# A three-layer kernel: the last two rows in another order, closing products by pair, conversions of the last layer placed elsewhere

## The chip, the cores and the metric

One core of one Trainium2 chip. The metric is the device time of one launch in microseconds (us), as the median of several runs; the profile is of one further execution. The engines have the names of the profile: PE (TensorE, matmuls), ACT (ScalarE), DVE (VectorE), POOL (GpSimd), SP (SyncE, which here only issues DMAs). PSUM is the memory that matmuls write to, in eight banks. Each engine works through its own instructions in the order in which the program issues them; what an instruction needs from another engine it waits for, and everything behind it on its engine waits too.

## The reference

Three layers, one behind the other. A delta-rule attention over 4 batches, 8 heads, 768 positions, heads of 48:

```python
for t in range(S):
    kt, vt, bt = (k_n[:, :, t], v[:, :, t], beta[:, :, t, None])
    y[:, :, t] = np.einsum('bhd,bhde->bhe', q[:, :, t], state)
    v_old = np.einsum('bhde,bhd->bhe', state, kt)
    state = state + bt[:, :, :, None] * np.einsum('bhd,bhe->bhde', kt, vt - v_old)
```

Its output, 3072 tokens of 384, goes through a gated layer of width 1536 (with an RMS norm ahead):

```python
g = xn @ w_gate
silu = g * (1.0 / (1.0 + np.exp(-g)))
return (silu * (xn @ w_val) @ w_out).astype(np.float32)
```

and that through a layer of width 2048 with h * tanh(softplus(h)) between its two products:

```python
h = x @ w_in
sp = np.where(h > 20.0, h, np.log1p(np.exp(np.minimum(h, 20.0))))
return ((h * np.tanh(sp)) @ w_out).astype(np.float32)
```

## The kernel before

**Products in three parts.** Every large product is taken as three matmuls: a number is split into a high part (rounded to the type of the fast fp32 matmul) and a low part (the rest), and high x high, high x low, low x high are summed in PSUM. So each operand exists as a pair of tiles: xh and xl, hh and hl, gh and gl, and wh and wl for each weight.

**Conversions.** The weights arrive as 64-bit floats. `prepare_half` (L150) turns one half of a weight block (128 x 384) into high and low parts, in steps between which other work is issued: a DMA to `raw` (four buffers); an abs pass into `t` (three buffers), on ACT (L166) or, with `act=False`, on DVE (L168); a pair of DVE passes (L170, L173); a second pair (L178, L181); then a cast to the high part, on ACT (L192) or DVE (L194), and the subtraction that gives the low part (L195), on the engine `low`, which is POOL unless a caller says otherwise. The subtraction is the last reader of `t`, so the abs pass three halves later waits for it. `convs` (L199) runs many halves one behind the other, overlapped by a step, and yields a weight for each step: 1.5 for each half, 0.3 at the start.

**Order by merging.** The program's order of issue is made by generators. `merge` (L61) takes streams with a total each and always continues the one whose done share of its total is smallest; `budget` (L71) ends a stream after an amount of weight; `run` issues streams one behind the other. A total that is larger than the stream's true weight lets it run ahead of the others.

**Phase b1: attention and the first third of the gated layer.** The sequence is worked through in 12 rows of 64 positions (256 tokens over the batches). `chain_row` (L891) issues one row as named stages: r (residual with the state), q0 and q1 (transposes of q), p (scores), y (output from the state), v (values: its results are copied by ACT into `ve`, L965, and it then loads the next row's v on SP, L395), k (update of the state sx, L1014; nothing in the last row), o0 and o1 (outputs: a product of `ve` and the scores into two banks, ACT copies `po`, L984, a sum of squares, and POOL's norm `rv`, L996), s0 and s1 (a diagonal matrix `dg` from `rv` on ACT, L1022), x0 and x1 (product with `dg`, L1036, six ACT copies to xh and xf, L1040 and L1042, POOL's xl, L1043; x1 also stores xh and xl to DRAM by SP). The capitals S, T, X, Y are s0, s1, x0, x1 of the row before, which the list of a row may place among its own stages. `ROW` is the list of rows 3 to 11; n, c and g prepare row r + 4 and issue nothing in the last four rows. Behind row 11 its own s0, s1, x0, x1 are issued by `run` (L1190).

Among the stages of row r the merge places 11 units of `part_a`, the gated layer on two pairs of weight blocks (`FA` = 2, L1135), some blocks behind the attention, and, in rows 10 and 11, conversions of the other weights. `gated` (L258): for each block of 256 tokens and each pair of weights four units (two pg, two pv, nine matmuls each), ACT's silu (L289), DVE's product sg and cast hh (L295, L298), POOL's hl (L299). Behind the first pair of a block come the closing products of the block before: `down` (L262), 12 matmuls for each of three output slices o, over both pairs of weights, then a copy of the slice by ACT (`par`, L1092). The slices use one PSUM bank in the rows, and three from L1192 on. Behind row 11 22 units are left ("the turns" below); they are merged with the conversions (L1194).

**Phase b2: the other pairs of the gated layer** (`phase_b2`, L1200), with the rest of the conversions of the last layer's weights but five (L1238 to 1241). The five, w_out2 blocks 3 to 7, are prepared with `act=False` and started in the last 14 units (L1244), up to an amount `CVC`.

**Phase c: the last layer** (`phase_c`, L1248). Units (n, m): 18 matmuls into a bank ph, ACT's sigmoid, arctan and sine, DVE's product t (L1307) and cast gh (L1310), POOL's gl (L1311). Units go in batches of three, the first batch before the last closing products of b2. Six banks hold ph; DVE's product t frees one. Behind each batch conversions of weight `CVD` are issued. `down` (L1254) closes a block of eight units with 96 matmuls, and needs all eight w_out2 blocks.

Of the kernel before, what the change touches and what calls it, by code (L numbers as in the profile page):

```python
# [8 lines left out]
F32 = mybir.dt.float32  # L9
# [8 lines left out]


P = dict(  # L20
    XB=2, WE=16, RB=4, TB=3, LANE=15.7, CVT=12.22, CVB0=0, CVB1=1.238, CVC=2.31, PSD=1, NU=6, CVA=1, CVE=14.671, CVD=4.076, SQ=5,
    ROW="r nA q0 q1 S p T nB y X v Y k c0 o0 c1 o1 g".split(),
    R0="r q0 q1 p v k o0 o1 s0 s1 x0 x1 c0 c1 g".split(),
    R1="r nA q0 q1 y p nB v k o0 o1 s0 s1 x0 c0 c1 g".split(),
    R2="r nA Y q0 q1 p nB y v k c0 o0 c1 o1 g".split(),
    DUE=[0, 6, 5, 11],
    CVS=[0, 0, 6.5, 0],
    C=dict(n=0.2, q=0.5, r=1.4, y=1.1, p=1.2, v=1.2, o=0.9, k=1.2, s=0.1, x=0.45, c=0.4, d=0.4, g=1.2, h=1.2),
# [69 lines left out]
def kernel(  # L98
# [14 lines left out]
    nc = tc.nc  # L113
    B, H, S, D = q.shape
    NT, DM = out.shape
# [142 lines left out]
    def gated(pools, pairs, blocks, get_x, finish_of, ahead=lambda n: None, between=lambda: None):  # L258
        ps_u, ps_d, hp, tp = pools
        pairs = list(pairs)  # L260

        def down(hs, finish):  # L262
            for o in range(KD):
                ps = ps_d[-1].tile([128, DM], F32, tag="d", name="pd")[:, 0:T]
                sl = slice(o * 128, (o + 1) * 128)
                for i, m in enumerate(pairs):
                    wh, wl = W["o", m]
                    hh, hl = hs[i]
                    for f in range(2):
                        last = i == len(pairs) - 1 and f == 1  # L270
                        nc.tensor.matmul(ps, wh[:, f, sl], hh[:, f, :], start=(i + f == 0), stop=False)  # L271
                        nc.tensor.matmul(ps, wh[:, f, sl], hl[:, f, :], start=False, stop=False)  # L272
                        nc.tensor.matmul(ps, wl[:, f, sl], hh[:, f, :], start=False, stop=last)  # L273
                    if i % 2 == 1 and i < len(pairs) - 1:
                        yield 1
                finish(o, ps)
                yield 1

        prev = None
        for n in blocks:  # L280
            hs = []
            for m in pairs:
                xh, xl = get_x(n)
                pg = ps_u.tile([128, 2, T], F32, tag="u", name="pg")
                up(pg, W["g", m], 0, xh, xl)
                yield 1
                up(pg, W["g", m], 1, xh, xl)
                sg = tp.tile([128, 2, T], F32, tag="sg", name="sg", bufs=2)
                nc.scalar.activation(out=sg, in_=pg, func=ACTF.Silu)  # L289
                yield 1  # L290
                pv = ps_u.tile([128, 2, T], F32, tag="u", name="pv")
                up(pv, W["v", m], 0, xh, xl)
                yield 1
                up(pv, W["v", m], 1, xh, xl)
                nc.vector.tensor_tensor(out=sg, in0=sg, in1=pv, op=ALU.mult)  # L295
                hh = hp.tile([128, 2, T], F32R, tag="hh", name="hh")
                hl = hp.tile([128, 2, T], F32R, tag="hl", name="hl")
                nc.vector.tensor_copy(hh, sg)  # L298
                nc.gpsimd.tensor_tensor(out=hl, in0=sg, in1=hh.bitcast(F32), op=ALU.subtract)  # L299
                hs.append((hh, hl))  # L300
                yield 1
                if m == pairs[0] and prev is not None:
                    yield from down(*prev)
                if m == pairs[1]:
                    ahead(n + 1)
            done.add(("up", n))
            prev = hs, finish_of(n)
        between()
        yield from down(*prev)

    def x_tiles():
        return [xp.tile([128, KD, T], F32R, tag=tag, name=tag, bufs=XB) for tag in ("xh", "xl")]
# [7 lines left out]
    def phase_b1():  # L320
# [759 lines left out]
            return P["C"][LATE.get(name, name)[0]]  # L1080

        def order(r):
            return P[f"R{r}"] if r < 3 else P["ROW"]

        def cost(r):
            return sum(cost_of(x) for x in order(r))
# [71 lines left out]
        for sg in range(1, NSEG):  # L1158
            for rl in range(2):
                r = 2 * sg + rl  # L1160
                streams = [(chain_row(r), cost(r))]
                due = P["DUE"][r] if r < len(P["DUE"]) else P["DUE"][-1]
                if due > 0:
                    off = 1.5 if r == 2 else 0
                    streams.append((seq(delay(off), budget(part_a, due)), off + due))
                if r < len(P["CVS"]):
                    streams.append((budget(cv, P["CVS"][r]), P["CVS"][r]))
                if r < len(P["CVS"]):
                    streams.append((budget(cv, P["CVS"][r]), P["CVS"][r]))
                if sg + 1 < NSEG:  # L1170
                    upto = (r - 1) * P["LANE"] - 1.5 if r < NR - 3 else 999.0
                    streams.append((until(lane, laned, upto), P["LANE"]))
                elif rl == 0:
                    st_i.close()
                    streams.append((seq(left.pop(), delay(7.0)), 13.0))
                    wbp.append(st_b.enter_context(pool("wbA")))
                    todo = [(c, m, cols(w, m)) for m in range(FA, NP1) for c, w in (("g", w_gate), ("v", w_val))]
                    todo += [("o", m, rows(w_out1, m)) for m in range(FA, NP1)]
                    gens = []
                    for i, (c, m, cut) in enumerate(todo):  # L1180
                        if 2 * i < WE:
                            gens.append(prepare(lambda: wbp[0], (c, m), cut, tag="wb", bufs=WE))
                        else:
                            gens.append(prepare(lambda: wbp[1], (c, m), cut, tag="wb", bufs=2 * len(todo) - WE))
                    cv = convs(gens)
                    streams.append((budget(cv, 0.75 * WE), 0.75 * WE))
                else:
                    streams.append((budget(cv, 0.75 * WE), 0.75 * WE))
                merge(*streams)
        run(*[late[x]() for x in LATE.values() if x in late])  # L1190
        st_a.close()
        ps_ds.append(st_p.enter_context(pool("ps_t", 3, space=PSUM)))  # L1192
        wbp.append(st_w.enter_context(pool("wbB")))
        merge((part_a, 22.0), (budget(cv, P["CVT"]), P["CVT"]))  # L1194
        st_p.close()
        st_m.close()
        return cv
# [2 lines left out]
    def phase_b2(cv, between):  # L1200
        st = ExitStack()
        op = st.enter_context(pool("op2", 1, side="right"))
        hp = st.enter_context(pool("hp2", NP1 - FA + 1, side="right"))
        tp = st.enter_context(pool("tp2", side="right"))
        pars = {}

        def load_par(n, o):
            pars[n, o] = op.tile([128, T], F32, tag="par", name="par", bufs=3)
            nc.scalar.dma_start(out=pars[n, o], in_=p_d[n][:, o, :])

        def next_x(n):
            if n < NR:
                load_x(n)
            else:
                load_x(0, (yh_d, yl_d))

        def finish_b(n):
            for o in range(KD):
                load_par(n, o)
            yh = op.tile([128, KD, T], F32R, tag="yh", name="yh")  # L1220
            yl = op.tile([128, KD, T], F32R, tag="yl", name="yl")

            def finish(o, ps):
                y = pars.pop((n, o))
                nc.vector.tensor_tensor(out=y, in0=y, in1=ps, op=ALU.add)
                nc.vector.tensor_copy(yh[:, o, :], y)
                nc.gpsimd.tensor_tensor(out=yl[:, o, :], in0=y, in1=yh[:, o, :].bitcast(F32), op=ALU.subtract)
                if o == KD - 1:
                    nc.sync.dma_start(out=yh_d[n], in_=yh.bitcast(F32))
                    nc.sync.dma_start(out=yl_d[n], in_=yl.bitcast(F32))  # L1230

            return finish

        more = [prepare(lambda: w2i, ("i", m), cols(w_in2, m)) for m in range(NP2)]
        more += [prepare(lambda: w2i, ("q", m), rows(w_out2, m)) for m in range(QE)]
        cv = seq(cv, convs(more))
        nb = NP1 - FA
        part_b = gated((ps_u, [ps_d], hp, tp), range(FA, NP1), range(NR), lambda n: xs[n], finish_b, next_x, between)  # L1238
        total = NR * 4 * nb + (NR - 1) * 6 - 4 * nb + 8
        merge((budget(part_b, 6), 6), (budget(cv, P["CVB0"]), 6))  # L1240
        merge((budget(part_b, total - 6), total), (cv, P["CVB1"] * 2.9 * (len(more) + 1)))
        cv = convs([prepare(lambda: wbp[0], ("q", m), rows(w_out2, m), act=not P["CVA"], tag="wb", bufs=WE) for m in range(QE, NP2)])
        rest.append(cv)
        merge((part_b, 4 * nb - 2), (budget(cv, P["CVC"]), P["CVE"]))  # L1244
        st.close()
# [122 lines left out]
```

## Time and profile before

| | us |
|---|---|
| median of 3 runs | 1226.76 (1225.94 to 1229.17) |
| the profiled execution | 1225.7 |
| its span, first to last instruction | 1224.0 |
| PE busy | 1128.9 (92%) |
| DVE busy | 707.6 (58%) |
| ACT busy | 566.8 (46%) |
| POOL busy | 418.1 (34%) |

The profile is of one execution. A busy time counts what an engine worked on; a line gives the engine, the line of the kernel, the tile written and the tiles read. An idle time in square brackets is that of the engine before the instruction, with what ended it. The granted clock is a mean over a stretch of the PE clock, as a share of 2.4 GHz; the chip has two levels, 2.4 and 1.2 GHz.

### The profile page before, as it was taken

What the parts mean: (1) busy time and instruction counts of PE and PEld (TensorE: products, weight loads), DVE (VectorE), ACT (ScalarE), POOL (GpSimd) and SP (SyncE); (2) the same over time, 40 slices, a digit from 0 to 9 for tenths busy, and PEclk for the clock granted to TensorE, in tenths of its full rate; (3) what the DMA queues carried; (4) which work ended last, traced back from release to release, by engine and by line L of the source; (5) the groups of instructions that cost most, each with busy time, mean ns of one, the idle gap of its engine ahead of it and who ended that gap; (6) DMA issues with size and microseconds to landing.
All of it is one profiled execution on the core that took longest, in us unless ns stands there. A gap on an engine that the chain in (4) does not pass through costs nothing.

```text
span 1224.0 us, 33707 instructions
## 1 busy us (share of the span) xinstructions
PE 1128.9 (92%) x14784; PEld 1098.7 (90%) x14784; DVE 707.6 (58%) x1130; ACT 566.8 (46%) x1075; POOL 418.1 (34%) x378
## 2 busy tenths in 40 slices
PE   5687698999998778999999999988999999999998
PEld 5676687989898678999999999988999999999998
DVE  6656898788877758455555542357434433343333
ACT  4355645565656563211211111163757555555672
POOL 2031135354322445334434442234323332232232
PEclk7666798999898989999999999998999999999999
DMA  9022233333224543434333231421111101111101
GB/s 159 3 67 67 80 80 67 81 88 85 55 80 119 144 143 130 130 116 143 104 118 103 86 110 65 142 91 52 40 39 40 40 14 39 40 40 39 37 4 27
DMA packets 120484, 95.08 MB, mean 78 GB/s; under 512 B 79856, under 2 KB 102896, under 8 KB 120336
## 3 DMA queue, kind: packets, MB, share of 16 engines
q1 hardware_dynamic: 108240, 69.32, 21.0%
q10 hardware_dynamic: 12096, 23.60, 5.8%
q8 instruction: 116, 1.90, 0.6%
q14 instruction: 32, 0.26, 0.1%
HBM read 64.59 MB, written 28.31 MB: 76 GB/s over the span
## 4 chain that ended last, share of the span: by engine, by line
PE 69%; DVE 18%; ACT 5%; issue 4%; POOL 2%; SPq 1%; DMA 1%; DVEq 0%; POOLq 0%; ACTq 0%
PE pd L1264 5%; PE pd L1265 5%; PE pd L1263 5%; PE ph L256 5%; PE ph L255 5%; PE ph L254 5%; PE pd L271 4%; PE pd L272 3%; PE pd L273 3%; PE pg L254 3%; PE pv L254 3%; PE pg L255 3%; PE pg L256 3%; PE pv L256 3%; PE pv L255 3%
## 5 line engine op out<-in xcount | busy, mean ns | idle before, releaser
L1311 POOL TENSOR_TENSOR gl<-t,gh 128x512 fp32r<-128x512 f32 x96 | 125.2, 1304 | 252.9 <-DVE gh L1310 237.6
L299 POOL TENSOR_TENSOR hl<-sg,hh 128x512 fp32r<-128x512 f32 x72 | 97.3, 1352 | 231.1 <-DVE hh L298 222.4
L254 PE MATMUL ph<-xh,wih 128*128 128x256 f32 x576 | 162.7, 283 | 5.4 <-DVE t L1307 5.4
L255 PE MATMUL ph<-xl,wih 128*128 128x256 f32 x576 | 162.5, 282 | 0.0
L256 PE MATMUL ph<-xh,wil 128*128 128x256 f32 x576 | 162.5, 282 | 0.0
L271 PE MATMUL pd<-hh,woh 128*128 128x256 f32 x432 | 126.0, 292 | 14.8 <-ACT par L1092 12.3
L1263 PE MATMUL pd<-wqh,gh 128*128 128x384 f32 x384 | 130.1, 339 | 1.9 <-DVE wqh L194 1.9
L1264 PE MATMUL pd<-wql,gh 128*128 128x384 f32 x384 | 130.4, 340 | 1.3 <-POOL wql L195 1.3
L1265 PE MATMUL pd<-wqh,gl 128*128 128x384 f32 x384 | 129.9, 338 | 0.0
L254 PE MATMUL pg<-xh,wgh 128*128 128x256 f32 x432 | 128.4, 297 | 0.5 <-ACT wgh L192 0.5
L289 ACT ACTIVATE sg<-pg 128x512 f32<-128x512 f32 x72 | 43.2, 599 | 183.4 <-PE pg L256 162.1
L254 PE MATMUL pv<-xh,wvh 128*128 128x256 f32 x432 | 126.7, 293 | 0.0
L255 PE MATMUL pg<-xl,wgh 128*128 128x256 f32 x432 | 124.1, 287 | 1.7 <-POOL xl L1043 1.7
L272 PE MATMUL pd<-hl,woh 128*128 128x256 f32 x432 | 123.9, 287 | 1.0 <-POOL hl L299 1.0
L256 PE MATMUL pg<-xh,wgl 128*128 128x256 f32 x432 | 123.9, 287 | 0.9 <-DVE wgl L195 0.9
L273 PE MATMUL pd<-hh,wol 128*128 128x256 f32 x432 | 123.6, 286 | 0.0
L255 PE MATMUL pv<-xl,wvh 128*128 128x256 f32 x432 | 122.4, 283 | 0.0
L256 PE MATMUL pv<-xh,wvl 128*128 128x256 f32 x432 | 122.2, 283 | 0.0
L254 PEld LDWEIGHTS ph<-xh,wih 128*128 128x128 f32 x576 | 109.7, 191 | 5.6 <-DVE t L1307 5.6
L295 DVE TENSOR_TENSOR sg<-sg,pv 128x512 f32<-128x512 f32 x72 | 49.2, 684 | 113.3 <-PE pv L256 103.1
L1307 DVE TENSOR_TENSOR t<-t,ph 128x512 f32<-128x512 f32 x96 | 65.2, 679 | 81.8 <-ACT t L1305 81.8
L255 PEld LDWEIGHTS ph<-xl,wih 128*128 128x128 f32 x576 | 109.8, 191 | 0.0
(207 smaller groups left out, 2918.2 us busy)
## 6 DMA issues: line engine op xcount, KB each, us to landing
raw<-in_moe_w_out_dram SPq DMA_DIRECT2D x28, 384.0 KB, 3.5
raw<-in_moe_w_in_dram SPq DMA_DIRECT2D x16, 384.0 KB, 3.8
kh<-in_k_dram SPq DMA_DIRECT2D x24, 192.0 KB, 3.9
qp<-in_q_dram SPq DMA_DIRECT2D x24, 192.0 KB, 3.5
v<-in_v_dram SPq DMA_DIRECT2D x48, 96.0 KB, 3.1
raw<-in_moe_w_gate_dram SPq DMA_DIRECT2D x12, 384.0 KB, 3.2
raw<-in_moe_w_val_dram SPq DMA_DIRECT2D x12, 384.0 KB, 3.4
xh_d<-xh SPq DMA_DIRECT2D x12, 384.0 KB, 2.8
```

The costliest lines, as they stand in the source:

```text
L254: nc.tensor.matmul(ps[:, f, :], wh[:, kt, sl], xh[:, kt, :], start=(kt == 0), stop=False)
L255: nc.tensor.matmul(ps[:, f, :], wh[:, kt, sl], xl[:, kt, :], start=False, stop=False)
L256: nc.tensor.matmul(ps[:, f, :], wl[:, kt, sl], xh[:, kt, :], start=False, stop=(kt == KD - 1))
L271: nc.tensor.matmul(ps, wh[:, f, sl], hh[:, f, :], start=(i + f == 0), stop=False)
L272: nc.tensor.matmul(ps, wh[:, f, sl], hl[:, f, :], start=False, stop=False)
L273: nc.tensor.matmul(ps, wl[:, f, sl], hh[:, f, :], start=False, stop=last)
L299: nc.gpsimd.tensor_tensor(out=hl, in0=sg, in1=hh.bitcast(F32), op=ALU.subtract)
L1263: nc.tensor.matmul(ps, gh[:, f, sl], wh[:, f, :], start=(m + f == 0), stop=False)
L1264: nc.tensor.matmul(ps, gh[:, f, sl], wl[:, f, :], start=False, stop=False)
L1265: nc.tensor.matmul(ps, gl[:, f, sl], wh[:, f, :], start=False, stop=last)
L1307: nc.vector.tensor_tensor(out=t, in0=t, in1=ps, op=ALU.mult)
L1311: nc.gpsimd.tensor_tensor(out=gl, in0=t, in1=gh.bitcast(F32), op=ALU.subtract)
```

## The change

`RL`, a new list of stages, is used in rows 10 and 11. It leaves out the names that issue nothing there, puts Y ahead of v, and o0 ahead of k. The closing products of the last block of part_a are issued by pair of weights: three banks are taken at once, pair 0 is multiplied for all three slices, then pair 1. Behind row 11 come s0 and s1, then three units of part_a, then x0 and x1; the conversions among the turns end earlier (`CVT` 9.0 instead of 12.22, and one weight of nothing behind them), and what is left of them goes into phase b2. For w_out1 blocks 2 to 5 and w_out2 blocks 3 to 7 the low part is made by DVE instead of POOL. In the last 14 units of b2 conversions of weight 4.4 instead of 2.31 are issued, behind a batch of phase c 3.5 instead of 4.076.

```diff
@@ -18,11 +18,12 @@
 
 
 P = dict(
-    XB=2, WE=16, RB=4, TB=3, LANE=15.7, CVT=12.22, CVB0=0, CVB1=1.238, CVC=2.31, PSD=1, NU=6, CVA=1, CVE=14.671, CVD=4.076, SQ=5,
+    XB=2, WE=16, RB=4, TB=3, LANE=15.7, CVT=9.0, CVB0=0, CVB1=1.238, CVC=4.4, PSD=1, NU=6, CVA=1, CVE=14.671, CVD=3.5, SQ=5,
     ROW="r nA q0 q1 S p T nB y X v Y k c0 o0 c1 o1 g".split(),
     R0="r q0 q1 p v k o0 o1 s0 s1 x0 x1 c0 c1 g".split(),
     R1="r nA q0 q1 y p nB v k o0 o1 s0 s1 x0 c0 c1 g".split(),
     R2="r nA Y q0 q1 p nB y v k c0 o0 c1 o1 g".split(),
+    RL="r q0 q1 S p T y X Y v o0 k o1".split(),
     DUE=[0, 6, 5, 11],
     CVS=[0, 0, 6.5, 0],
     C=dict(n=0.2, q=0.5, r=1.4, y=1.1, p=1.2, v=1.2, o=0.9, k=1.2, s=0.1, x=0.45, c=0.4, d=0.4, g=1.2, h=1.2),
@@ -259,6 +260,23 @@
         ps_u, ps_d, hp, tp = pools
         pairs = list(pairs)
 
+        def down_by_pair(hs, finish):
+
+            pss = [ps_d[-1].tile([128, DM], F32, tag="d", name="pd")[:, 0:T] for _ in range(KD)]
+            for i, m in enumerate(pairs):
+                wh, wl = W["o", m]
+                hh, hl = hs[i]
+                for o, ps in enumerate(pss):
+                    sl = slice(o * 128, (o + 1) * 128)
+                    for f in range(2):
+                        last = i == len(pairs) - 1 and f == 1
+                        nc.tensor.matmul(ps, wh[:, f, sl], hh[:, f, :], start=(i + f == 0), stop=False)
+                        nc.tensor.matmul(ps, wh[:, f, sl], hl[:, f, :], start=False, stop=False)
+                        nc.tensor.matmul(ps, wl[:, f, sl], hh[:, f, :], start=False, stop=last)
+                    if i == len(pairs) - 1:
+                        finish(o, ps)
+                    yield 0.5
+
         def down(hs, finish):
             for o in range(KD):
                 ps = ps_d[-1].tile([128, DM], F32, tag="d", name="pd")[:, 0:T]
@@ -306,7 +324,7 @@
             done.add(("up", n))
             prev = hs, finish_of(n)
         between()
-        yield from down(*prev)
+        yield from (down_by_pair if len(pairs) == FA else down)(*prev)
 
     def x_tiles():
         return [xp.tile([128, KD, T], F32R, tag=tag, name=tag, bufs=XB) for tag in ("xh", "xl")]
@@ -1080,7 +1098,7 @@
             return P["C"][LATE.get(name, name)[0]]
 
         def order(r):
-            return P[f"R{r}"] if r < 3 else P["ROW"]
+            return P[f"R{r}"] if r < 3 else P["RL"] if r >= NR - 2 else P["ROW"]
 
         def cost(r):
             return sum(cost_of(x) for x in order(r))
@@ -1181,17 +1199,20 @@
                         if 2 * i < WE:
                             gens.append(prepare(lambda: wbp[0], (c, m), cut, tag="wb", bufs=WE))
                         else:
-                            gens.append(prepare(lambda: wbp[1], (c, m), cut, tag="wb", bufs=2 * len(todo) - WE))
+                            gens.append(prepare(lambda: wbp[1], (c, m), cut, low=nc.vector, tag="wb", bufs=2 * len(todo) - WE))
                     cv = convs(gens)
                     streams.append((budget(cv, 0.75 * WE), 0.75 * WE))
                 else:
                     streams.append((budget(cv, 0.75 * WE), 0.75 * WE))
                 merge(*streams)
-        run(*[late[x]() for x in LATE.values() if x in late])
+        last = [x for x in LATE.values() if x in late]
+        run(*[late[x]() for x in last if x[0] == "s"])
+        run(budget(part_a, 3))
+        run(*[late[x]() for x in last if x[0] == "x"])
         st_a.close()
         ps_ds.append(st_p.enter_context(pool("ps_t", 3, space=PSUM)))
         wbp.append(st_w.enter_context(pool("wbB")))
-        merge((part_a, 22.0), (budget(cv, P["CVT"]), P["CVT"]))
+        merge((part_a, 19.0), (seq(budget(cv, P["CVT"]), delay(1)), P["CVT"] + 1))
         st_p.close()
         st_m.close()
         return cv
@@ -1239,7 +1260,7 @@
         total = NR * 4 * nb + (NR - 1) * 6 - 4 * nb + 8
         merge((budget(part_b, 6), 6), (budget(cv, P["CVB0"]), 6))
         merge((budget(part_b, total - 6), total), (cv, P["CVB1"] * 2.9 * (len(more) + 1)))
-        cv = convs([prepare(lambda: wbp[0], ("q", m), rows(w_out2, m), act=not P["CVA"], tag="wb", bufs=WE) for m in range(QE, NP2)])
+        cv = convs([prepare(lambda: wbp[0], ("q", m), rows(w_out2, m), low=nc.vector, act=not P["CVA"], tag="wb", bufs=WE) for m in range(QE, NP2)])
         rest.append(cv)
         merge((part_b, 4 * nb - 2), (budget(cv, P["CVC"]), P["CVE"]))
         st.close()
```

## Rows read from the trace of the kernel before

**Rows 1.** The page: the granted clock of PE in 40 equal slices (tenths).

```profile
PEclk7666798999898989999999999998999999999999
```

**Rows 2.** Stretches, all engines: length, busy time (instructions) by engine, granted clock, DMA share, GB/s.

```profile
408.00:458.30 50.30, 35.93 (x495) 33.08 (x493) 34.84 (x58) 27.52 (x78) 24.59 (x26) 0.87 0.46 143
458.30:491.00 32.70, 29.09 (x227) 28.49 (x226) 27.28 (x40) 12.99 (x34) 15.70 (x13) 0.94 0.36 122
491.00:806.20 315.20, 315.20 (x2648) 315.20 (x2647) 154.43 (x264) 58.58 (x106) 117.56 (x107) 1.00 0.34 111
...
818.90:834.00 15.10, 9.67 (x58) 9.52 (x57) 12.17 (x24) 11.47 (x18) 6.38 (x6) 0.77 0.31 96
834.00:856.60 22.60, 19.39 (x97) 17.97 (x96) 15.87 (x32) 5.39 (x8) 10.22 (x9) 0.92 0.11 40
```

**Rows 3.** Timeline of PE: start, duration, line, tiles, [idle before <- what ended it].

```profile
414.36 1.55 PE L976 MATMUL pp<-ve,PT 128*64 128x96 f32 x16 [2.37 <-ACT po L984]
...
427.43 0.39 PE L271 MATMUL pd<-hh,woh 128*128 128x256 f32 x1 [3.73 <-ACT par L1092]
...
444.31 1.08 PE L976 MATMUL pp<-ve,PT 128*64 128x96 f32 x16 [1.83 <-ACT po L984]
...
455.64 2.93 PE L1036 MATMUL pp<-dg,po 128*128 128x128 f32 x12 [5.52 <-ACT dg L1022]
...
484.58 0.38 PE L271 MATMUL pd<-hh,woh 128*128 128x256 f32 x1 [2.56 <-DVE hh L298]
...
824.48 0.58 PE L254 MATMUL ph<-xh,wih 128*128 128x256 f32 x1 [5.43 <-DVE t L1307]
```

**Rows 4.** Timeline of ACT in row 11.

```profile
435.79 0.56 ACT L166 ACTIVATE t<-raw 128x384 f32<-128x384 f32 x1 [1.37 <-POOL wgl L195]
436.35 0.89 ACT L1040 ACTIVATE xh<-pp,gT 128x128 fp32r<-128x128 f32 x3
...
437.86 1.95 ACT L965 COPY ve<-pp 64x384 f32<-64x384 f32 x4
...
440.33 0.50 ACT L192 CAST wvh<-t 128x384 fp32r<-128x384 f32 x1
```

**Rows 5.** Timeline of POOL in row 11, and its last conversion in the last layer.

```profile
444.12 1.07 POOL L1043 TENSOR_TENSOR xl<-xf,xh 128x384 fp32r<-128x384 f32 x1 [2.20 <-ACT xf L1042]
...
446.58 1.00 POOL L195 TENSOR_TENSOR wvl<-t,wvh 128x384 fp32r<-128x384 f32 x1
447.55 1.29 POOL L299 TENSOR_TENSOR hl<-sg,hh 128x512 fp32r<-128x512 f32 x1
...
852.98 2.02 POOL L195 TENSOR_TENSOR wql<-t,wqh 128x384 fp32r<-128x384 f32 x2 [1.75 <-DVE wqh L194]
```

**Rows 6.** DVE: three places of its timeline, then groups by form (busy us, mean ns | idle), 807 to 857.

```profile
483.39 0.68 DVE L295 TENSOR_TENSOR sg<-sg,pv 128x512 f32<-128x512 f32 x1
484.10 0.43 DVE L298 CAST hh<-sg 128x512 fp32r<-128x512 f32 x1
...
823.75 0.68 DVE L1307 TENSOR_TENSOR t<-t,ph 128x512 f32<-128x512 f32 x1
...
L181 DVE SCALAR_TENSOR_TENSOR t<-raw,t 128x384 int32<-128x384 int32 x9 | 7.9, 881 | 0.3
...
L178 DVE SCALAR_TENSOR_TENSOR t<-raw,t 128x384 int32<-128x384 int32 x9 | 6.1, 677 | 0.2
L173 DVE TENSOR_SCALAR t<-t 128x384 int32<-128x384 int32 x8 | 3.6, 444 | 0.3
L194 DVE CAST wqh<-t 128x384 fp32r<-128x384 f32 x10 | 3.4, 351 | 0.0
...
L168 DVE TENSOR_SCALAR t<-raw 128x384 int32<-128x384 int32 x7 | 2.5, 360 | 7.9 <-POOL wql L195 7.9
```

**Rows 7.** Low halves on DVE, early in the run (ns min/median/max), and POOL beside one.

```profile
L195 DVE TENSOR_TENSOR wol<-t,woh x4: 546/548/1556, 149.4 to 161.7; 128x384 fp32r<-128x384 f32 x4
...
159.89 1.48 POOL L538 TENSOR_TENSOR kh<-kh,rn 128x768 f32<-128x768 f32 x1 [1.08 <-DVE rn L537]
```

## The prediction

> **What bounds the kernel now.** I read the page first. TensorE (PE) is busy for 92% of the span, and its granted clock is high except at the start, with a few dips later [rows 1]. So time can only come from where PE stands idle, or runs at the lower of its two clock levels (1.2 instead of 2.4 GHz). The table by stretches finds these places [rows 2]. From 491.0 to 806.2 us (the middle layer) PE never idles and the granted clock is 1.00: nothing can be won there, and the end follows at once whatever is won before. The other stretches lose time:
> - The last two rows, 408.0 to 458.3: 50.30 - 35.93 = 14.4 us idle; at a mean clock of 0.87, 50.30 x 0.13 = 6.5 us more go to the low level.
> - The turns behind them, 458.3 to 491.0: 3.6 us idle, 32.70 x 0.06 = 2.0 us of clock.
> - The start of the last layer, 818.9 to 856.6: 5.4 + 3.2 = 8.6 us idle, 15.10 x 0.23 + 22.60 x 0.08 = 5.3 us of clock.
>
> Together 40 us, the most that this change could take. The list of PE's waits names what ends each [rows 3]: in the rows ScalarE (ACT), with copies that PE needs; at the turns VectorE's (DVE's) hh of the last pair; in the last layer DVE's product t, which frees a PSUM bank.
>
> The queues in front of these say why. ACT's abs pass of a weight conversion needs a t buffer (three rotate) that POOL's low half must first release, so one late POOL operation holds up everything behind that pass in ACT's queue. In the last layer DVE idles 7.9 us in seven waits for the same POOL low halves, each in front of work that PE needs [rows 6].
>
> **The change, part by part.** Following the merges weight by weight gives the order of issue before and after; that of before agrees with the trace. The steps below compare places in these two orders.
>
> *Rows 10 and 11, order.* The empty stages drop out, so a row's cost is 10.0, not 12.4, and the row is spread over all of its window.
>
> Gone: in row 10 the second output product waited for copies (2.4 us, [rows 3]). Now pg, the k update, a second pg and a pv lie between, 4.4 us of products. Row 11's last wait, for dg (5.5 us), shrinks: three units of gated work now run before to_x. ACT needs from the last output's end about 7.3 us to the first par copy behind dg (2.1 us that it is behind, then copies, casts and an abs at half a microsecond each, and POOL's rv and low half in between [rows 4, 5]); PE has 5.5 us of work, so 1.8 remain.
>
> Unchanged: in row 11 the second closing product waits for a par copy behind an abs pass behind POOL (3.7 us); the order there is the same, only one transpose moved out of it: 4.0. Then scores follow q1 directly and wait for its copy, 0.6. Row 11's second output waits 1.5 instead of 1.8, since k issues nothing in the last row.
>
> New: Y now stands before v. The ve copies then stand on ACT behind a cast (0.50), an abs that waits for POOL's xl (1.07) and low half (1.00), and Y's six copies (2 x 0.89, start to start 1.5); the first half of ve adds 1.0 [rows 4, 5]. That is 5.1 us from the end of X's copies; PE arrives after 2.5. So a wait of 2.6 at the first output, in both rows.
>
> Sum of PE waits: 2 x 2.6 + 4.0 + 0.6 + 1.5 + 1.8 = 13.1 against 14.4; the clock would fall as often. By PE that gains 1.3. By ACT's queue, which is what PE waits for, the point behind both to_x and the first two closing products comes 5.5 us sooner. I take 3.0, between the two. Bounds: -4, if the two new waits come on top, and +9, if they are covered. Y's stores to DRAM now stand on SP ahead of the loads of the last v: those land some 5 us later, and are needed 4 us later still; nothing.
>
> *Closing products by pair.* The matmuls are the same. Before, PE stood 2.6 us for hh, then for hl [rows 3], because DVE began its product late, behind conversion passes: at 483.39, while PE had stopped at 482.02, six matmuls after pv's last [rows 3, 6], so some 2 us. Now the 18 products of pair 0 come first: 18 x 0.119 (315.20 / 2648, [rows 2]) = 2.1 us of cover. DVE's product, cast and POOL's hl take 0.68 + 0.43 + 1.29 = 2.4 [rows 5, 6]; with half a microsecond of delay 0.8 remain. DVE is less late because 5.5 halves, not 7, stand before: a half's four passes take 0.35 + 0.44 + 0.68 + 0.88 = 2.35 by the means of [rows 6] (the first as the cast of equal size beside it), so 7 x 2.35 = 16.5 falls to 12.9, plus four low halves moved from POOL at 0.55 [rows 7] = 15.1. Of the 5.6 us lost in this stretch I take 4.2 back. Bounds: 1.5, if DVE is as late as before and the clock falls, and 5.6. The conversions left over (about two halves) go into the middle layer, where PE is full and DVE is busy 154 of 315 us: nothing, as long as the last output weights are there at its first closing product; they are issued right before, with 18 products of cover.
>
> *Last layer.* More passes run while DVE is idle at the end of the middle layer (the second pair of q3's second half, a cast, a low half, a whole q4 half), and the low halves run on DVE.
> - First wait. DVE reached unit 0.3's product at 823.75. Three of the seven waits go (7.9 x 3/7 = 3.4), one pair of passes goes (0.68 + 0.88 = 1.6), three low halves come (3 x 0.55 = 1.7): 3.3 us sooner. Bounds 0 and 5.4.
> - Weights for the first output. The last low half ended at 852.98 + 2.02 = 855.0 [rows 5]. All seven waits go (7.9), passes moved out 1.6 + 0.35 + 0.36 + 2.35 = 4.6, the last pair on POOL 2.0, nine low halves come (5.0): 845.5. PE's 96 matmuls start 3.3 us sooner, and what is left of them at 834 is 19.39 - 1.8 (clock) = 17.6 us of work: 834.0 - 3.3 + 17.6 = 848.3 instead of 856.6. The last weights are read some 2 us before the end, so they are just in time.
>
> Gain 8.3; bounds 4 and 11.
>
> Here a rule must be weighed. One low half on DVE took 1.556 us against 0.548 typically [rows 7]: it ran beside a POOL operation of 1.48. The Trainium skill (SBUF — State Buffer, Who interferes with whom) says that a DVE instruction with two SBUF inputs and a POOL instruction that reads SBUF exclude each other, the second to issue blocking fully; that one row agrees. By the rule each low half may wait for a gl, and the gain would be small (the second rival).
>
> **Sum.** 3.0 + 4.2 + 8.3 = 15.5 us. The profiled execution took 1225.7 (span 1224.0), the median of the runs is 1226.76, 1.06 above. So 1210.2 in a profile like this one, **1211.3** by the median.
>
> **The rivals.**
> - *The new waits at the first outputs win over the old ones.* For it: ve behind Y on ACT is plain in the order. Against: DVE and POOL have less before them there. Rows -4 instead of +3: 1226.8 - 8.5 = 1218.3.
> - *Low halves on DVE collide with POOL.* The nine in the last layer take up to 1.0 us more each (1.556 - 0.548), and gl, hl are on POOL all the time. The three in front of unit 0.3 take back 3.0 of 3.3; the last weights come at 854.5; the layer gains about 1 instead of 8.3: 1226.8 - 8.2 = 1218.6. Against: the other halves of that weight ran at about 0.55 [rows 7]. This is the rule of the Trainium skill named above.
> - *Nothing arrives at the end*: the waits go elsewhere in the same stretches, 1226.8.
> - *Slower: the clock stays low through both rows.* Six waits of 0.6 to 4 us, a few microseconds apart, could hold PE at 1.2 GHz from 408 on. For it: slices 2 to 4 of the page, with short work and waits, were granted 0.6 [rows 1]. Against: before, with four long waits there, the mean was 0.87. Price: PE work of 35.93 - 6.5 = 29.4 us takes 58.8; with the 13.1 of waits 72 us instead of 50.3, so +21.6, less the other 12.5: 1235.9. It decides once the rows lose over 12.5 + 3.7 = 16.2 us.
>
> **How the numbers follow.** 0.3% (3.7 us) is about what a measurement of this kernel can tell from no change. Forecast 0.62; new waits 0.14; collisions 0.12; nothing 0.06; slower 0.06. The first three are faster: 0.88; same 0.06; slower 0.06. The low end is the upper bounds together, 9 + 5.6 + 11 = 25.6: 1201. The high end takes in both faster rivals and a few microseconds more: 1222. Left out are the last two cases and a little of the others, under 2 in 10.
>
> **What would show it.** Right: no PE wait for hh at the last closing products beyond 1 us; no DVE wait for wql; PE's wait for t near 2 us and none for wql; the dg wait under 2.5 us; a new PE wait for ve at the first output. Wrong: a clock mean under 0.8 in the rows; low halves on DVE near 1.5 us; the middle layer no longer at full PE (late weights); or PE waiting for hh as before, because low halves on DVE wait for ACT's casts in front of it.

## The result and the profile after

The changed kernel takes 1212.0 us (median of 4, 1208.25 to 1214.92), the kernel before 1226.35 in runs beside it: a ratio of 0.9885, 95% interval 0.9869 to 0.9901. It is faster, and 0.7 us from the 1211.3 forecast. The profiled span fell from 1224.0 to 1211.1.

Row 10 does not begin at the same microsecond in each execution (below), so stretches are compared by the same work: from row 10's first matmul to the second closing product behind to_x; the rest of the turns; the middle layer; the last layer up to its first output. First the kernel before, by stretches in the columns of [rows 2], without the middle layer, which [rows 2] has; then the one after.

```profile
378.00:462.44 84.44, 65.70 (x1199) 61.06 (x1199) 55.12 (x89) 49.67 (x125) 35.30 (x39) 0.88 0.44 129
462.44:491.03 28.59, 24.98 (x195) 24.38 (x194) 24.74 (x37) 9.94 (x23) 12.86 (x11) 0.94 0.38 125
806.22:856.57 50.35, 41.71 (x260) 40.09 (x259) 38.24 (x72) 23.17 (x33) 23.36 (x20) 0.90 0.22 71
```

```profile
379.70:461.79 82.09, 65.96 (x1198) 61.32 (x1198) 57.12 (x91) 47.53 (x117) 34.91 (x37) 0.86 0.42 128
461.79:486.55 24.76, 23.56 (x195) 23.36 (x195) 18.00 (x33) 11.94 (x31) 7.41 (x6) 0.98 0.48 160
486.55:801.74 315.19, 315.19 (x2648) 315.19 (x2647) 164.42 (x282) 58.53 (x107) 116.38 (x105) 1.00 0.35 112
801.74:843.92 42.18, 38.54 (x260) 37.13 (x259) 39.36 (x73) 23.06 (x33) 12.73 (x10) 0.96 0.23 76
```

The same PE instructions (the counts agree) take 2.35 us less in the rows, 3.83 less at the turns, nothing less in the middle layer, which is full in both, and 8.17 less in the last layer. Length minus PE's busy time is idle time: rows 18.7 to 16.1, turns 3.6 to 1.2, layer 8.6 to 3.6. A busy time that shrinks for the same work is clock: 1.4 us at the turns (granted 0.94 before, 0.98 after), 3.2 in the layer (0.90 and 0.96); in the rows it grew by 0.3. PE's timeline of the kernel after has these stalls, to be held against [rows 3]:

```profile
410.74 0.88 PE L994 MATMUL pp<-ve,PT 128*64 128x96 f32 x16 [2.60 <-ACT ve L983]
...
427.09 0.58 PE L289 MATMUL pd<-hh,woh 128*128 128x256 f32 x1 [4.30 <-ACT par L1110]
...
445.09 0.90 PE L994 MATMUL pp<-ve,PT 128*64 128x96 f32 x16 [2.71 <-ACT ve L983]
...
448.62 1.55 PE L994 MATMUL pp<-ve,PT 128*64 128x96 f32 x16 [0.41 <-ACT po L1002]
...
457.89 0.38 PE L289 MATMUL pd<-hh,woh 128*128 128x256 f32 x1 [1.77 <-ACT par L1110]
...
484.42 0.38 PE L274 MATMUL pd<-hl,woh 128*128 128x256 f32 x1 [1.20 <-POOL hl L317]
...
817.50 0.39 PE L255 MATMUL ph<-xh,wih 128*128 128x256 f32 x1 [2.93 <-DVE t L1328]
```

The two waits for ve are new; the wait for dg (5.52) has become 1.77 on the par copy behind dg; that for hh is gone and hl's is left. ACT's timeline of row 11 shows what ve stands behind:

```profile
442.13 0.54 ACT L167 ACTIVATE t<-raw 128x384 f32<-128x384 f32 x1 [1.81 <-POOL wvl L196]
442.58 0.87 ACT L1058 ACTIVATE xh<-pp,gT 128x128 fp32r<-128x128 f32 x3
443.32 0.89 ACT L1060 ACTIVATE xf<-pp,gT 128x128 f32<-128x128 f32 x3
444.07 1.95 ACT L983 COPY ve<-pp 64x384 f32<-64x384 f32 x4
```

An abs pass that waits for POOL's low half, then Y's six copies, then ve: the queue of the prediction, the idle time before the abs included. In the last layer DVE waits for no low half any more: its abs passes, which waited 7.9 us for POOL before [rows 6], now wait only for the load of a weight (us, times, longest; from 780 to 846).

```profile
DVE t L169 <- DMA raw<-in_moe_w_out_dram: 2.8, 2, 1.7
```

The low halves that it makes itself there (a line by source, ns min/median/max), and one of them with the POOL operations (a group of two) that it ran beside:

```profile
L196 DVE TENSOR_TENSOR wql<-t,wqh x10: 557/560/1562, 788.9 to 841.8; 128x384 fp32r<-128x384 f32 x10
```

```profile
808.04 1.53 DVE L196 TENSOR_TENSOR wql<-t,wqh 128x384 fp32r<-128x384 f32 x1
```

```profile
806.50 2.66 POOL L1332 TENSOR_TENSOR gl<-t,gh 128x512 fp32r<-128x512 f32 x2 [1.22 <-DMA yl_d<-yl]
```

Three of the ten took 1.53 to 1.56 us, each beside a gl or hl of POOL; the others 0.56. Such collisions are not new in the layer. In the kernel before POOL's gl met DVE's conversion passes in the same place, right behind a batch's products:

```profile
811.01 1.65 DVE L178 SCALAR_TENSOR_TENSOR t<-raw,t 128x384 int32<-128x384 int32 x1
812.69 1.53 DVE L181 SCALAR_TENSOR_TENSOR t<-raw,t 128x384 int32<-128x384 int32 x1
```

Leaving the gh casts aside, which stretch to 1.0 us five times in each kernel, the layer up to its first output has five stretched DVE operations before (1.65, three of 1.52 to 1.53, one of 1.03) and four after (a wqh cast of 1.48, two wql of 1.53, a pass of 1.54).

### The profile page after: what moved, and what is told of

It reads as the page before. It is cut to its first block, busy times and chain, and to the rows that moved or that the text cites. A ratio compares the mean times of both kernels' runs of the same rounds, so it can differ in the third digit from the quotient of the medians.

```text
span 1211.1 us, 33707 instructions
## 1 busy us (share of the span) xinstructions
PE 1125.3 (93%) x14784; PEld 1095.4 (90%) x14784; DVE 713.1 (59%) x1148; ACT 566.7 (47%) x1075; POOL 400.4 (33%) x360
## 4 chain that ended last, share of the span: by engine, by line
PE 70%; DVE 17%; ACT 5%; issue 4%; POOL 2%; DMA 1%; SPq 1%; DVEq 0%; POOLq 0%; ACTq 0%
PE pd L1285 5%; PE pd L1286 5%; PE pd L1284 5%; PE ph L256 5%; PE ph L257 5%; PE ph L255 5%; PE pd L289 4%; PE pg L255 4%; PE pd L291 4%; PE pd L290 3%; PE pg L257 3%; PE pg L256 3%; PE pv L255 3%; PE pv L256 3%; PE pv L257 3%
## 5 line engine op out<-in xcount | busy, mean ns | idle before, releaser
L289 PE MATMUL pd<-hh,woh 128*128 128x256 f32 x420 | 122.3, 291 | 15.0 <-ACT par L1110 15.0
L290 PE MATMUL pd<-hl,woh 128*128 128x256 f32 x420 | 119.7, 285 | 0.0
L291 PE MATMUL pd<-hh,wol 128*128 128x256 f32 x420 | 119.6, 285 | 0.0
L1328 DVE TENSOR_TENSOR t<-t,ph 128x512 f32<-128x512 f32 x96 | 65.2, 679 | 82.1 <-ACT t L1326 82.1
```

The lines of the kernel that those rows point to most:

```text
L1328: nc.vector.tensor_tensor(out=t, in0=t, in1=ps, op=ALU.mult)
```

## The experiments

Each ratio is to the kernel before, run on the same chip in turn, with its 95% interval. "Rows and turns" is from row 10's first matmul to the end of the turns: 113.0 us before, 106.9 after; "layer" is the last stretch above: 50.4 and 42.2. How far such a length repeats is seen where the code of a stretch is the same: rows and turns of before and e3 113.0 and 113.2, of after and e7 to e10 106.7 to 108.0; the layer of after, e4 to e6, e9 and e11 42.1 to 42.2, of before, e1 and e2 50.4 to 50.9. Differences below 1.3 us in the first, 0.6 in the second, are not read.

**Three parts, each alone.** e1 has only the list of stages, e2 only the turns (products by pair, units ahead of to_x, low halves of w_out1 on DVE, amounts there), e3 only the last layer.

```diff
# e1: before, and
+    RL="r q0 q1 S p T y X Y v o0 k o1".split(),
-            return P[f"R{r}"] if r < 3 else P["ROW"]
+            return P[f"R{r}"] if r < 3 else P["RL"] if r >= NR - 2 else P["ROW"]
# e2: after, and RL unused; w_out2 low halves on POOL, CVC=2.31, CVD=4.076
# e3: before, and w_out2 low halves on DVE, CVC=4.4, CVD=3.5
```

> The kernel before with the new order of rows 10 and 11 alone. By my steps the two waits for ve (2.6 us each) appear and the 2.4 us wait of row 10 goes, but without the three units ahead of to_x the wait for dg stays at 4 us or more: 0 to 2 us faster than before, inside what can be told from no change. Rival (the order of the rows carries the 3 us of the sum by itself): 3 us faster, with the wait for dg under 2.5 us.

> The kernel before with the turns of the change alone: products by pair, three units ahead of to_x, fewer conversions, low halves of w_out1 on DVE. Mine: the stretch of the turns 3.8 us shorter, and some 2 us more from the wait for dg, which the units now cover in part: 5 to 6 us faster. Rival (the turns gain only because the new row order leaves ACT less behind): under 3 us.

> The kernel before with the conversions of the last layer alone (low halves on DVE, 4.4 and 3.5). Mine: the start of the last layer 8.2 us shorter, the kernel 8.2 us faster, and nothing changed before 780 us. Rival (part of the 8.2 us comes from the earlier stages reaching it differently): 5 us or less.

| | time | ratio | rows and turns | layer |
|---|---|---|---|---|
| e1 | 1229.35 | 1.0016 (1.0003 to 1.0030) | 115.6 | 50.8 |
| e2 | 1221.61 | 0.9962 (0.9948 to 0.9977) | 108.4 | 50.9 |
| e3 | 1218.65 | 0.9938 (0.9916 to 0.9960) | 113.2 | 42.2 |

e3 came as expected, e2 gained 4.7 to 5.1 us where 5 to 6 were expected, and e1 missed both its expectation and its rival, which had the order gaining. The layer adds to the rest: 42.2 whatever stands ahead. The other two parts do not simply add: the order alone costs 2.4 to 2.6 us in rows and turns, the turns alone gain 4.7, both gain 5.0 to 6.4 (106.7 to 108.0). So beside the turns the order makes a difference of 0.4 to 1.7, which by the measure above is not shown to be a gain; without them it costs. The stretch up to the end of to_x, then from there to the end of the turns, in the kernel before and in e1:

```profile
378.00:458.22 80.22, 61.48 (x1165) 56.84 (x1165) 52.58 (x85) 46.54 (x115) 32.47 (x36) 0.87 0.45 130
458.22:491.03 32.81, 29.20 (x228) 28.60 (x228) 27.28 (x40) 13.07 (x34) 15.70 (x13) 0.94 0.36 121
```

```profile
378.26:459.81 81.55, 63.55 (x1165) 58.93 (x1165) 52.18 (x85) 46.99 (x115) 33.07 (x36) 0.83 0.42 127
459.81:493.89 34.08, 31.19 (x227) 30.79 (x227) 26.67 (x40) 13.18 (x34) 15.12 (x13) 0.85 0.34 117
```

Up to to_x idle time is 18.7 and 18.0, the same 1165 instructions take 2.1 us longer at a clock of 0.83 for 0.87, and the stretch is 1.3 us longer. Behind it idle time is 3.6 and 2.9, the same products take 2.0 us longer at 0.85 for 0.94, and the stretch is again 1.3 longer. So e1 waits less in both and works longer: its loss shows as lower clock, not as waits. Whether a lower clock lengthens the rows is seen where the code is the same, as in the rows of the changed kernel, of e8 and of e9 (the latter two below, to be held against the first row of the stretches after):

```profile
380.06:462.10 82.04, 64.54 (x1198) 60.00 (x1198) 57.26 (x91) 47.50 (x117) 34.85 (x37) 0.88 0.42 128
375.84:459.07 83.23, 67.23 (x1198) 62.54 (x1198) 57.08 (x91) 47.64 (x117) 34.76 (x37) 0.84 0.41 126
```

In e8 PE worked 1.4 us less than in the changed kernel and waited 1.4 us more (the par wait that was 1.77 is 3.37), so the higher clock gained nothing there. In e9 PE worked 1.3 us more, waited as long, and the rows are 1.1 us longer. So a lower clock can be taken up by shorter waits, and it can lengthen the rows; why e1's was lower stays open. The waits of e1 by what ended them (us, times, longest):

```profile
PE pp L977 <- ACT ve L966: 5.3, 2, 2.7
PE pd L272 <- ACT par L1093: 4.3, 1, 4.3
PE pp L1037 <- ACT dg L1023: 3.6, 1, 3.6
```

The new ve waits stand in place of those for po (4.2 before), and the wait for dg is still 3.6: it takes the units of the turns to cover it (e6 below). With the turns and the old order (e2) the stretch to the second closing product behind to_x is 83.69, hardly shorter than the 84.44 before:

```profile
376.72:460.41 83.69, 67.38 (x1198) 62.78 (x1198) 57.49 (x91) 47.19 (x117) 34.30 (x37) 0.84 0.41 125
```

**v ahead of Y.** Are the new waits for ve a cost?

```diff
-    RL="r q0 q1 S p T y X Y v o0 k o1".split(),
+    RL="r q0 q1 S p T y X v Y o0 k o1".split(),
```

> The changed kernel with v ahead of Y again in rows 10 and 11. If the waits for ve cost what PE shows, both (2.60 and 2.71 us) go and the kernel is 3 to 5 us faster than the changed one. Rival (ACT's queue sets the rows, and the wait only moves behind it): the same within 1.5 us, with a longer wait at the second output or at the closing products.

1214.49 us, ratio 0.9898 (0.9880 to 0.9916), rows and turns 109.8. PE's waits in the rows:

```profile
PE pg L255 <- ACT xh L1058: 5.7, 2, 3.0
PE pg L256 <- POOL xl L1061: 3.8, 2, 2.0
...
PE pp L994 <- ACT ve L983: 2.5, 2, 1.3
```

By the ratios it is 1.6 us slower than the changed kernel, with intervals that overlap, and not 3 to 5 faster; rows and turns are 1.8 to 3.1 us longer. The waits for ve halve (2.8 us less), and 9.5 us come at the units that read Y's copies, against 2.8 us less for par: the copies stand on ACT one behind the other, and which is first only says who waits. So the new waits are a price of the order, but not one that another place of v avoids.

**By slice, and to_x first.** Two parts of the turns undone, one at a time.

```diff
# e5
-        yield from (down_by_pair if len(pairs) == FA else down)(*prev)
+        yield from down(*prev)
# e6
-        run(*[late[x]() for x in last if x[0] == "s"])
-        run(budget(part_a, 3))
-        run(*[late[x]() for x in last if x[0] == "x"])
+        run(*[late[x]() for x in last])
# (and part_a's total 22.0 again)
```

> The changed kernel with the last closing products of part_a by slice again (all else as changed). Mine: only 6 products instead of 18 cover DVE's and POOL's 2.4 us, so PE waits 2.5 to 3 us in place of 1.2 and the clock falls behind it: the turns 2 to 3.5 us longer. Rival (the turns gained because fewer conversions stand on DVE before the last product): under 1 us longer.

> The changed kernel with to_x ahead of the three units again. The order of the rows alone made rows and turns 2.6 us longer, the turns alone 4.7 us shorter, both together 6.2 us shorter. If the missing 4 us hang on the three units (they cover the wait for dg, which the new order makes start later), this kernel has a wait for dg of 3.5 us or more and rows and turns 3 to 5 us longer than the changed one. Rival (they hang on the conversions moved out of the turns): under 2 us longer.

e5: 1215.12 us, 0.9912 (0.9889 to 0.9935), rows and turns 109.6; e6: 1214.73, 0.9905 (0.9878 to 0.9932), 110.8. In e5 PE waits twice at the last closing products, in e6 it waits for dg as in e1 (one list of waits of each):

```profile
PE pd L290 <- POOL hl L317: 1.2, 1, 1.2
PE pd L289 <- DVE hh L316: 1.2, 1, 1.2
```

```profile
PE pp L1054 <- ACT dg L1040: 3.5, 1, 3.5
```

For e5 the turns alone can be read, from the second closing product behind to_x on: 27.2 us, against 24.5 to 24.8 in the five executions with the changed code, and 28.6 before. So the pairs are worth 2.5 us, as expected. The other 1.4 are put down to the fewer conversions in front of hh (hh 1.2 in e5, 2.56 before); no run has these alone. The units ahead of to_x are worth 2.8 to 4.1 (110.8 against 106.7 to 108.0), also as expected. The times alone do not tell e5 or e6 from the changed kernel, whose interval theirs overlap.

**The two parts of the last layer.** e7: low halves of w_out2 on POOL again; e8: the amounts of before (CVC=2.31, CVD=4.076).

> The changed kernel with the low halves of w_out2 on POOL again, the amounts 4.4 and 3.5 kept. Mine: DVE's waits of 1.1 us for POOL come back, some seven, less nine low halves of 0.55: the last weights 3 to 5 us later, the start of the last layer 4 to 6 us longer. Rival (the amounts alone do it): under 2 us longer.

> The changed kernel with the amounts of before (2.31 and 4.076), the low halves of w_out2 on DVE kept. Mine: about one and a half halves more stand on DVE in the last layer (4.6 us with one contended pair): its start 3 to 5 us longer. Rival (the engine alone does it): under 2 us longer.

e7: 1216.84 us, 0.9930 (0.9910 to 0.9949), layer 46.1; e8: 1216.80, 0.9927 (0.9906 to 0.9948), layer 46.2. Undoing the low halves loses 3.9 of the 8.2 us, undoing the amounts 4.0: each part brings about half, and neither rival holds. In e7 DVE waits seven times for POOL again, 12.3 us in all from 780 on, where it was 7.9 before. In e8 it doesn't, and PE waits for t and for the last weights. First DVE in e7, then PE in e8:

```profile
DVE t L169 <- POOL wql L196: 12.3, 7, 3.4
```

```profile
PE ph L255 <- DVE t L1328: 4.0, 1, 4.0
...
PE pd L1284 <- DVE wqh L195: 1.9, 2, 1.4
```

**What holds the last wait for t, 2.93 us?** Behind the first batch the t tiles rotate so that unit 0.3 takes that of unit 0.2, and ACT's sigmoid waits 3.8 us for POOL's gl. e9 gives it a fresh one; e10 also moves conversions to ahead of the layer.

```diff
# e9
-        ts = ts[3:] + [tp.tile([128, 2, T], F32, name=f"t{i}") for i in (4, 5)] + ts[:3]
+        ts = ts[:1] + [tp.tile([128, 2, T], F32, name=f"t{i}") for i in (4, 5)] + ts[1:]
# e10: e9, and CVC=7.4, CVD=2.6
```

> The changed kernel, but unit 0.3 of the last layer takes a fresh t buffer instead of that of unit 0.2, so that ScalarE's sigmoid no longer waits 3.8 us for POOL's gl. What holds the last wait of TensorE for t (2.9 us at 817.5 in the changed kernel)? Theory, VectorE's queue: VectorE worked without a gap from 801.9 to 816.8 and reached the product only then, the first sine ended about 814.3; an earlier sine gives nothing: t wait 2.9, layer 42.2, time as the changed kernel (within 1 us). Rival, the chain of ScalarE: the product follows the sine, 3.8 us sooner: t wait under 1, layer about 39 to 40, 2 to 3 us less.

> The same fresh buffer, and again more of the last layer's weight conversions ahead of its first product (7.4 instead of 4.4 of the planner's units, then 2.6 instead of 3.5 behind each batch). Theory, VectorE's queue: 0.9 of 1.5 units, so 0.6 of a half of 3 us, is gone ahead of unit 0.3's product and about one half more is done before the layer: 2 to 5 us sooner, and the sine, sooner too, allows it: t wait 0 to 1, the clock stays high, layer 38 to 40, time 2 to 4 us less than the changed kernel. Rival: the conversions that are moved ahead wait for weight buffers that the middle layer still reads, or delay its last closing work: layer 42 or more, no gain.

e9: 1212.27 us, 0.9894 (0.9867 to 0.9920), layer 42.2. ACT's first sine now starts at 809.03, DVE's product comes at 814.06, PE has waited as long as before:

```profile
814.79 0.38 PE L255 MATMUL ph<-xh,wih 128*128 128x256 f32 x1 [2.94 <-DVE t L1328]
```

So DVE's queue sets it, not ACT's chain, and the theory of e9 holds. e10: 1214.29 us, 0.9905 (0.9885 to 0.9924). Its layer is 37.1 us, 5.1 shorter, but the middle layer grew from 315.2 to 323.9. DVE and PE at the end of the middle layer:

```profile
797.55 0.56 DVE L182 SCALAR_TENSOR_TENSOR t<-raw,t 128x384 int32<-128x384 int32 x1
798.02 0.68 DVE L313 TENSOR_TENSOR sg<-sg,pv 128x512 f32<-128x512 f32 x1
```

```profile
799.22 0.39 PE L289 MATMUL pd<-hh,woh 128*128 128x256 f32 x1 [4.38 <-DVE hpi L1309]
```

The moved conversions stand in front of the last sg and hh, and PE stops for 4.4 us where it had never stopped; from 793.0 to 809.5 its clock averages 0.79. (The list names the memset hpi, which ended right behind hh; what PE reads is hh.) This is the second form of e10's rival, the middle layer's last closing work delayed; the layer itself did shorten as its theory said. The idle time of DVE lies behind that hh, not ahead of it.

**All low halves of the middle layer on DVE.** Rows 10 and 11 still have POOL's. The waits of the changed kernel, ACT's from 379 to 462, DVE's from 379 to 487:

```profile
ACT t L167 <- POOL wgl L196: 10.8, 7, 2.2
ACT t L167 <- POOL wvl L196: 10.7, 6, 3.4
```

```profile
DVE t L171 <- ACT t L167: 16.7, 10, 4.6
```

```diff
-                            gens.append(prepare(lambda: wbp[0], (c, m), cut, tag="wb", bufs=WE))
+                            gens.append(prepare(lambda: wbp[0], (c, m), cut, low=nc.vector, tag="wb", bufs=WE))
```

> The changed kernel, but all low halves of the middle layer's weights on VectorE, those in rows 10 and 11 too. In the changed kernel ScalarE waits there for POOL's low halves (wgl 10.8, wvl 10.7 us), VectorE for ScalarE's abs passes 16.7 us, and TensorE for ScalarE's copies (par 6.1, ve 5.3). Theory, ScalarE's queue sets the rows and POOL's low halves hold that queue: the ve and par waits fall by half or more, rows and turns 106.9 become 101 to 104, time 3 to 6 us less than the changed kernel. Rival, VectorE becomes the bound (12 low halves of 0.6 to 1.5 us more in its queue, each behind a cast of ScalarE): new waits of TensorE for VectorE's PT or hh, rows and turns 106 to 109, no gain.

1205.70 us, 0.9837 (0.9819 to 0.9854): by the ratios 5.9 us faster than the changed kernel, where 3 to 6 were expected; rows and turns are 99.4, below the 101 to 104 expected. The rows, PE's waits in them, and ACT's for the low halves, which are DVE's now:

```profile
380.59:455.78 75.19, 62.79 (x1198) 58.28 (x1198) 56.58 (x104) 46.94 (x115) 16.70 (x22) 0.91 0.46 139
```

```profile
PE pp L994 <- ACT ve L983: 4.1, 2, 2.0
...
PE pd L289 <- ACT par L1110: 1.9, 2, 1.4
```

```profile
ACT t L167 <- DVE wvl L196: 7.8, 6, 2.2
ACT t L167 <- DVE wgl L196: 6.6, 6, 2.0
```

82.1 us have become 75.2: idle 16.1 to 12.4, busy 66.0 to 62.8 at a clock of 0.91 for 0.86. The waits for par fall from 6.1 to 1.9, those for ve only from 5.3 to 4.1. DVE does 13 instructions more there and is busy no longer (56.6 us, 57.1 in the changed kernel). ACT's waits for low halves were 22.5 us in the rows of the kernel before and 21.5 in the changed one; here they are 14.4, and the rows are shorter by about as much (6.9). So ACT's queue sets the rows, POOL's low halves held that queue, and the new order of the stages hardly touched this. Whether it is the shorter subtraction (0.55 us on DVE, 1.0 to 1.1 on POOL) or the work that stood ahead of it on POOL was not told apart.

**Both.** e12 is e11 with the fresh t tile, and with one half of a conversion moved from behind the first batch to right behind the last hh.

```diff
         nc.vector.memset(hpi, 1.5707963267948966)
+        early = rest[-1]
...
         held = begin(units[0:NBATCH])
+        for _ in budget(early, 1.5):
+            pass
         yield
...
-            for _ in budget(rest[-1], P["CVD"]):
+            for _ in budget(rest[-1], P["CVD"] - (0 if i else 1.5)):
```

> The kernel with all low halves of the middle layer's weights on VectorE (1205.7 us), and of the last layer: the fresh t buffer for unit 0.3, and one half of a conversion (1.5 units, 3.1 us of VectorE) moved from behind the first three products to right behind the last hh of the middle layer, where VectorE waits 3.1, 2.0 and 2.0 us for TensorE's closing products; what is issued by the end of each later batch stays. Theory, VectorE's queue sets the last t wait and its idle time is only behind the last hh, not ahead of it: t wait 2.9 becomes 0 to 0.5, the middle layer stays at 315.2, layer 42.1 becomes 37.5 to 40, time 1201 to 1204. Rival: the half delays the sums behind the closing products, and with them the PSUM banks that these need: TensorE waits up to 1 to 3 us there, and the gain is given back: 1204 to 1207.

1202.80 us, 0.9808 (0.9795 to 0.9821), the fastest kernel of the study and inside the expected 1201 to 1204. Its middle and last layers:

```profile
477.85:793.05 315.20, 315.20 (x2649) 315.20 (x2647) 168.22 (x289) 59.78 (x108) 116.34 (x105) 1.00 0.35 114
793.05:832.13 39.08, 37.33 (x261) 35.85 (x259) 36.43 (x66) 21.89 (x32) 12.77 (x10) 1.00 0.21 71
```

The middle layer keeps its length, the wait for t is gone, the clock is 1.00, and the layer is 3.1 us shorter. e10 had moved two halves (3.0 of weight) to ahead of the last hh; e12 moves one to right behind it. One half ahead of hh was not tried, nor this half without the fresh tile, which alone gave nothing (e9).

## Why the prediction was right

- **Rows, 3.0 taken, 2.35 measured**, and 1.2 to 2.4 over the six executions with this code up to there (rows of 82.0 to 83.2 us). The 3.0 was a choice between 1.3 and 5.5, so that it came close is in part luck. Of the single waits: ve 2.6 in both rows, measured 2.60 and 2.71; par 4.0, measured 4.30; row 11's second output 1.5, measured 0.41; behind dg 1.8, measured 1.77; scores for q1 0.6, no such wait. That the wait behind dg fits is luck: it was 1.77 and 1.78 in the changed code twice, 3.15 to 3.46 in e5, e7, e8 and e10, as PE came later or sooner. The step booked under the order a gain that it does not bring by itself: the order alone costs (e1), the rows with the units and the old order are 83.69 (e2), 0.5 to 1.7 above those of the changed code, and the dg wait goes with the units (e6). Its second reading, that by ACT's queue the rows end 5.5 us sooner, did not come; moving the low halves that ACT waits for brings such a gain (e11), shuffling ACT's queue does not.
- **Turns, 4.2 taken, 3.83 measured.** hl 0.8, measured 1.20. The lateness of DVE went as worked out: sg started at 483.39 before, 1.4 us behind PE's stop, and at 481.64 after, while pair 0's products ran (they began at 480.79). Pairs 2.5 (e5) and the rest of 1.4 make it up.
- **Last layer, 8.3 taken, 8.17 measured.** The first wait was sized too well: unit 0.3's product came 15.0 us after the layer's start instead of 17.5, 2.5 sooner and not 3.3, and PE waited 2.93 where some 2 was expected. Against that the clock gave 3.2 where 1.8 was taken, so the size of the sum is luck too, while its two causes are shown (e7, e8). The weights of the first output were just in time, as forecast: one wait of 0.46 for wqh.
- **The rivals.** The new waits did come and did not win, since others shrank by more: idle time fell from 18.7 to 16.1 (e4 shows that the new waits belong to ACT's queue). The collisions did come, at their price of 1.0 us each, but at 3 of 10 halves, one of them still in the middle layer. The trace agrees with the rule of the Trainium skill (SBUF — State Buffer, Who interferes with whom) in that only halves beside a POOL operation stretched. The collisions did not decide, for two reasons that the traces show. POOL was busy for 12.7 of the layer's 42.2 us, mostly right behind each batch's products, while DVE's conversions go on for longer. And a low half that collides stands where a conversion pass collided before, so the price was not new: five stretched operations before, four after. The slow rival's clock did not come: 0.86 over the rows, with 0.3 us more of PE's work. It came nearer than that mean tells: the last 52 us of them had 0.81, and the prediction's sign of being wrong was a mean under 0.8.

```profile
409.70:461.79 52.09, 41.85 (x584) 39.07 (x585) 37.04 (x59) 28.79 (x78) 26.82 (x27) 0.81 0.45 138
```

- **The sum.** The three stretches gain 14.35 us, the medians differ by 14.35 too, 15.5 were taken; the profiled spans differ by 12.9, because row 10 began 1.7 us later in the second. That it is so close is in part chance, by the scatter above.

What stays open: whether the new order of the stages helps at all beside the turns, or once POOL's low halves are gone (e11 with the old list was not tried), and why the clock is lower with the order alone.

## What to carry to other kernels

Where three engines hand a tile round in a ring, as the abs pass, the passes and the low half do here, look for the longest wait around the ring in the stage that is bound, and move the operation that others wait for, even to a busier engine: that gave more than the new order. Place filler work by what stands behind it in its queue: two halves in front of the last hh made PE wait 4.4 us, one half right behind it cost PE nothing. And a reordering is tried alone as well as beside the other parts: here it cost 2.6 us alone, and no gain beside them is shown, though the whole change gained.

## What was not expected of the hardware

The same program up to row 10 took from 374.4 to 380.6 us to reach it in the fourteen profiles of this study, while stretches behind it repeat to 1.3 us or better. So parts of a change are better read by the length of a stretch of equal work than by the total. And idle time and clock cannot simply be added up as losses: between e8 and the changed kernel the lower clock took from PE's waits what it added to PE's work, though between e9 and the changed kernel it did lengthen the rows.
